# Two layers of cached attention and a token mixer on one core: part of the weights' last query tile as two tiles of 64 rows

## The chip, the cores and the metric

The kernel runs on one core of a Trainium2 chip. The core has a matrix engine (PE, with its weight loads shown as PEld), a vector engine (DVE), an activation engine (ACT), GpSimd (POOL) and a sync engine (SP) that here does nothing but issue DMAs. Sixteen DMA engines bring data from HBM into the on-chip memory (SBUF, 128 partitions). The metric is the device time of one execution in microseconds (us); lower is better.

## The reference

A decode step for a batch of two tokens, in float32, through two identical layers. Each layer is an attention block over a long cache and a small mixer:

```python
def _A_ref(x, k_cache, v_cache, wq, wo):          # x (2, 1, 512)
    # 32 query heads of 128, 8 cached heads, 32768 keys
    q = (lambda x, *d: x.transpose(*d))((x @ wq).reshape(B, Sq, Hq, Dh), 0, 2, 1, 3)
    k = jnp.repeat(k_cache, rep, axis=1)
    v = jnp.repeat(v_cache, rep, axis=1)
    scores = jnp.einsum("bhqd,bhkd->bhqk", q, k) * (Dh ** -0.5)
    p = _softmax(scores, axis=-1)
    o = jnp.einsum("bhqk,bhkd->bhqd", p, v)
    return (lambda x, *d: x.transpose(*d))(o, 0, 2, 1, 3).reshape(B, Sq, Hq * Dh) @ wo
def _B_ref(x, w1, b1, w2, b2):                    # token mixer, 1792 hidden
    h = _layernorm(x, axis=-1)
    u = jnp.einsum("bsd,sf->bdf", h, w1) + b1
    u = _gelu(u)
    y = jnp.einsum("bdf,fs->bds", u, w2) + b2
    return (lambda x, *d: x.transpose(*d))(y, 0, 2, 1)
# both blocks twice, with the same weights and cache
x = x + _A_ref(_layernorm(x, axis=-1), A_k_cache, A_v_cache, A_wq, A_wo)
x = x + _B_ref(_layernorm(x, axis=-1), B_w1, B_b1, B_w2, B_b2)
```

K and V of one batch entry and one cached head are 16 MB each, 512 MB in all, and both layers read the same cache. The weights of one cached head (its four query heads' columns of wq, its rows of wo) are 2 MB.

## The kernel before

**Units.** The work is cut into 32 units (layer, batch entry, cached head). For each unit the kernel makes the query (`make_q`), multiplies it with eight chunks of K (`k_chunk`, L359), finds the maximum, takes exponentials, multiplies with eight chunks of V (`v_chunk`, L492), and adds the result, through wo, to a row sum (`out_1`, `out_2`, L190). A chunk is 2 MB: 128 partitions of 4096 floats. In most of the span K and V come in loads of four chunks, 8 MB; around the two changes of batch entry and layer (some 1000 to 1550 us) the loads are one or two chunks.

**Order.** The function body first writes down, at fixed places in the stream of chunks, which piece of work follows which chunk (`at(time, f, ...)`), and then walks the stream once: load, chunks, pieces that are due. Each engine runs its instructions in that order, so the order of the DMAs in SP's queue is the order in which `load_k` (L344), `load_v` (L446, and L433 for chunks that stay resident) and `load_weights` (L115) are called. Each load is one issue on SP. It waits for what last read or wrote its place in SBUF; whatever stands behind it in SP's queue waits with it.

**Memory.** `mem` holds 13 cells of 4096 floats per partition, and behind them a rest of 5 x 512. Cells 0 to 8 are the ring through which K and V pass: two buffers of four cells for loads of 8 MB. Cells 9 to 12 hold weights. The rest keeps five quads of one V chunk of head 7 between the layers, and at the end one output row.

**Weights.** Heads 5 and 7 are `RESIDENT`: loaded once and kept. The other six, `passing` = 0, 1, 2, 3, 4, 6, are loaded once in each layer. So there are 14 loads: head 0 at the start, the others ten chunks before the first K chunk of the unit that needs them (`at(kbeg[n] - 10, load_weights, ...)`). In the order of SP's queue such a load stands right behind a V load, and the next K load behind it. One load brings 128 rows of 16 KB: four tiles of wq (the 512 inputs as four times 128 partitions, 512 columns each), then four of wo. `wq_at` and `wo_at` give the tiles.

**The query.** `make_q` runs in three steps, two of two matmuls each (L292, the normalized input as the stationary side, one tile of wq as the moving side, 128 rows deep, added up in one PSUM bank) and one that turns the row into columns. The query of a passing head is made for both batch entries at once. The normalized input stands as columns in `xnT`, four for each batch entry, one for each tile of 128 inputs. `first_input` makes them for layer 0 from the loaded input, `to_columns` for layer 1.

Of the kernel before, what the change touches and what calls it, by code (L numbers as in the profile page):

```python
# [10 lines left out]
ALU = mybir.AluOpType  # L11
AX = mybir.AxisListType

P = 128
CK = 4096
# [20 lines left out]
DIRECT = 2  # L36
TAIL_GROUPS = (3, 3, 3, 2, 1)
IDLE = (4, 1, 3, 2)
EPS = 1e-5


@with_exitstack
def gqa_mixer_kernel(ctx: ExitStack, tc: tile.TileContext, x, kt, v, wqo, cols, out):
# [50 lines left out]

# [15 lines left out]
    def wo_at(h):  # L110
        return cells(home[h])[:, W:].rearrange("p (t c) -> p t c", t=R)

    def load_weights(h, cell):
        home[h] = cell
        nc.sync.dma_start(cells(cell), wqo[h])  # L115


    used = [0] * (WCELL0 + WCELLS + 1)
# [63 lines left out]
    def misc():  # L182

        turn[0] += 1
        return small[:, turn[0] % NG * P :][:, :P]
# [13 lines left out]
    def first_input():  # L199

        t = spot()
        cen, sq = (t[:, k * B * DT : (k + 1) * B * DT].rearrange("p (b d) -> p b d", b=B) for k in range(2))
        m, rs = (t[:, (2 * DT + k) * B : (2 * DT + k + 1) * B] for k in range(2))
        p = misc()
        nc.tensor.matmul(p[:, : B * DT], ones, xcols.rearrange("p b d -> p (b d)"), start=True, stop=True)
        nc.vector.tensor_reduce(m, p[:, : B * DT].rearrange("p (b d) -> p b d", b=B), axis=AX.X, op=ALU.add)
# [4 lines left out]
        p = misc()  # L211
        nc.tensor.matmul(p[:, : B * DT], ones, sq.rearrange("p b d -> p (b d)"), start=True, stop=True)
        nc.vector.tensor_reduce(rs, p[:, : B * DT].rearrange("p (b d) -> p b d", b=B), axis=AX.X, op=ALU.add)
        nc.vector.tensor_scalar(rs, rs, 1.0 / D, EPS, op0=ALU.mult, op1=ALU.add)
        nc.gpsimd.tensor_tensor(rs, rs, half_neg.to_broadcast([P, B]), op=ALU.pow)
        for b in range(B):
            xT[b] = xcols[:, b, :]
            nc.vector.tensor_scalar_mul(xnT[:, :, b], cen[:, b, :], rs[:, b : b + 1])  # L218

    *ends, keeper = RESIDENT  # L220
# [30 lines left out]
    def to_columns(key):  # L251

        layer, b = key
        pt = misc()
        for d in range(DT):
            nc.tensor.matmul(  # L256
                pt[:, d : d + 1], ysb[key][:, d * P : (d + 1) * P], ident[:, :1], start=True, stop=True
            )
        nc.vector.tensor_scalar_add(xT[b], pt[:, :DT], b2c)
        mv, rs = stats[key]  # L260
        nc.vector.tensor_scalar(  # L261
            xnT[:, :, b], pt[:, :DT], mv[:, 0:1], rs, op0=ALU.subtract, op1=ALU.mult
        )

    def unit_of(n):

# [10 lines left out]
    def make_q(n, step, place=None):  # L277


        layer, b, h = unit_of(n)  # L280
        both = partner(n)
        m = 1 if both is None else B
        if n in q_kept:
            if step == 2:
                nc.vector.tensor_copy(qpad[n % 2][:, 28 : 28 + R], q_kept.pop(n))
            return
        if step == 0:

            q_ps[n] = pfix.tile([P, 512], F32, name="bcast") if N1 < n <= N3 + 2 else kept[0]
        if step < 2:  # L290
            for d in range(step * DT // 2, (step + 1) * DT // 2):
                nc.tensor.matmul(  # L292
                    q_ps[n][:m, :],
                    xnT[:, d, b : b + m],
                    wq_at(h)[:, d, :],
                    start=(d == 0),
                    stop=(d == DT - 1),
                )
# [234 lines left out]
    def out_2(n):  # L533
        layer, b, h = unit_of(n)
        for r in range(R):
            add_row(r, b, oT[n][:, r, :], wo_at(h)[:, r, :])

    ysb, px = {}, {}
    slope, shift, stats = {}, {}, {}
# [81 lines left out]
    def last_mixer(n):  # L621
# [9 lines left out]
        for k, to in enumerate((kept[1], acc)):  # L631
            for r in range(R):
                nc.tensor.matmul(
                    to[32 * r : 32 * r + 1, :w],
                    oT[n][:, r, 1:],
                    wo_at(h)[:, r, k * w : (k + 1) * w],
                    start=True,
                    stop=True,
                    skip_group_check=True,
                )  # L640
# [81 lines left out]
    def mix_4(key):  # L722

        layer, b = key
        p = px[key]
        nc.tensor.matmul(p, sel[b], ysb[key], start=False, stop=True, skip_group_check=True)
        if layer == LAYERS - 1:
            y = mem[:1, (WCELL0 + WCELLS) * CK :][:, :D]
# [54 lines left out]
    for n in range(NU):  # L783
# [111 lines left out]
def _layout(A_x, A_k_cache, A_v_cache, A_wq, A_wo, B_w1, B_b1, B_w2, B_b2):  # L895

    import numpy as np

    B, HKV, SK, DH = A_k_cache.shape
    D = A_x.shape[-1]  # L900
    n = SK // CK


    keys = np.arange(SK).reshape(n, CK)
    for c0, m in GROUPS:
        keys[c0 : c0 + m] = keys[c0 : c0 + m].reshape(P, m, CK // P).transpose(1, 0, 2).reshape(m, CK)
    k = keys.reshape(n // PACK, PACK // 2, 2, NG, 32, JT // QT, QT // SUB, SUB)
    k = k.transpose(0, 1, 6, 7, 3, 2, 5, 4).reshape(n, CK)
    kt = np.empty((B * HKV, SK * DH), A_k_cache.dtype)
    for u, a in enumerate(A_k_cache.reshape(B * HKV, SK, DH)):  # L910
        for c0, m in GROUPS:
            kt[u, c0 * CK * DH : (c0 + m) * CK * DH] = a[k[c0 : c0 + m].ravel()].T.ravel()
    wq = A_wq.reshape(D // P, P, HKV, -1).transpose(2, 1, 0, 3)
# [4 lines left out]
    return {  # L918
        "x": np.ascontiguousarray(A_x.reshape(B * (D // P), P).T),
        "kt": kt,  # L920
        "v": A_v_cache.reshape(B * HKV, SK * DH),
        "wqo": np.concatenate([wq.reshape(HKV, P, -1), wo.reshape(HKV, DH, -1)], axis=2),
        "cols": np.concatenate(cols, axis=1),
    }

# [24 lines left out]
```

## Time and profile before

| | us |
|---|---|
| three runs: median (lowest to highest) | 2501.64 (2501.58 to 2502.9) |
| the profiled execution: its time | 2501.79 |
| the profiled execution: span from first to last instruction | 2500.0 |
| busy in the span: PE / PEld / DVE / ACT | 1383.1 / 375.5 / 222.4 / 185.4 |
| bytes read from HBM | 1065.91 MB, 426 GB/s over the span |

Lines of the profile name engine, line of the kernel, operation and "out<-in". The letter q behind an engine (SPq) means its sequencer: waits and DMA issues. "PE scores L359 <- DMA mem<-in_kt_dram" is PE at line 359 waiting for a K load; `in_v_dram` is V, `in_wqo_dram` the weights. A wait for several things is put down to the one that came last. "us to landing" is counted from a DMA's issue to its completion.

### The profile page before, as it was taken

Reading aid. Unit: us, or ns where it says so; the run is one execution under the profiler, and the core shown is the slowest. Engines: PE = TensorE matmul, PEld = TensorE weight load, DVE = VectorE, ACT = ScalarE, POOL = GpSimd, SP = SyncE. Lnnn points to the kernel's source line nnn. Section 1 sums busy time; section 2 is a strip of 40 time slices with the busy share of each in tenths; the row PEclk is TensorE's granted clock in tenths of the full one; section 3 lists DMA queues with packets and bytes.
Section 4 is the critical chain, followed back from the end, with each engine's and each line's share of the span. In section 5 each row is a group of like instructions: output and inputs, shape, how many; then the busy total and the mean of one; then the engine's idle time right before and its main releaser. Section 6 shows DMA issues by size and latency. Waiting matters only on the chain.

```text
span 2500.0 us, 20528 instructions
## 1 busy us (share of the span) xinstructions
PE 1383.1 (55%) x9326; PEld 375.5 (15%) x9326; DVE 222.4 (9%) x610; ACT 185.4 (7%) x550; POOL 4.9 (0%) x17
## 2 busy tenths in 40 slices
PE   4545554645445554657667775455546454455546
PEld 1111111111111111111111211111111111111112
DVE  0000000000000000001111110000000000010002
ACT  0000000000000000001012010000000000011002
POOL 0000000000000000000000000000000000000000
PEclk8777777877777777879888977677778777777778
DMA  9999999999999999999999999999999999999996
GB/s 419 436 433 430 433 435 430 436 430 430 433 433 431 434 429 435 425 423 421 426 427 427 423 430 430 432 435 434 432 430 435 435 423 435 433 433 426 432 429 292
DMA packets 31200, 1067.23 MB, mean 427 GB/s; under 512 B 3717, under 2 KB 3721, under 8 KB 4618
## 3 DMA queue, kind: packets, MB, share of 16 engines
q1 hardware_dynamic: 30824, 1065.89, 99.2%
q8 instruction: 73, 1.20, 0.2%
q14 instruction: 13, 0.11, 0.0%
q10 hardware_dynamic: 290, 0.04, 0.0%
HBM read 1065.91 MB, written 0.00 MB: 426 GB/s over the span
## 4 chain that ended last, share of the span: by engine, by line
DMA 74%; PE 24%; issue 0%; DVE 0%; ACT 0%; SPq 0%; POOL 0%; ACTq 0%
DMA mem<-in_v_dram 65%; PE acc L492 19%; DMA mem<-in_kt_dram 9%; PE scores L359 3%; PE bcast L292 1%; PE rows L190 0%; PE small L385 0%; PE small L521 0%; ACT S L714 0%; PE kept L671 0%; PE small L379 0%; PE small L256 0%; ACT mem L681 0%; ACT mem L693 0%; PE bcast L575 0%
## 5 line engine op out<-in xcount | busy, mean ns | idle before, releaser
L359 PE MATMUL scores<-mem,small_sb 128*32 128x512 f32 x4096 | 620.6, 722 | 592.0 <-DMA mem<-in_kt_dram 591.6
L492 PE MATMUL acc<-mem,S 128*16 128x512 f32 x4088 | 614.1, 738 | 468.2 <-DMA mem<-in_v_dram 462.5
L359 PEld LDWEIGHTS scores<-mem,small_sb 128*32 128x32 f32 x4096 | 151.1, 127 | 970.5 <-issue 895.5
L396 ACT ACTIVATE S<-S,small_sb 128x128 f32<-128x128 f32 x240 | 123.5, 519 | 2102.4 <-DVE small_sb L387 1636.6
L492 PEld LDWEIGHTS acc<-mem,S 128*16 128x16 f32 x4088 | 134.8, 110 | 831.7 <-issue 693.2
L369 DVE TENSOR_REDUCE small_sb<-scores 128x1 f32<-128x512 f32 x64 | 44.2, 691 | 874.1 <-PE scores L359 874.1
L391 DVE STREAM_TRANSPOSE S<-scores 128x512 f32<-128x512 f32 x64 | 45.4, 710 | 131.4 <-PE acc L492 131.4
L292 PE MATMUL kept<-mem,small_sb 128*2 128x512 f32 x104 | 50.9, 615 | 1.7 <-DVE small_sb L218 1.7
L190 PE MATMUL rows<-mem,small_sb 128*1 128x512 f32 (+1 forms) x276 | 48.4, 603 | 3.1 <-ACT mem L714 2.4
L396 ACT ACTIVATION_READ_ACCUMULATOR S<-S,small_sb 128x1 f32 x240 | 44.8, 187 | 0.0
L381 DVE TENSOR_REDUCE small_sb<-small 1x4 f32<-1x128 f32 x32 | 8.8, 276 | 280.7 <-PE small L379 280.7
L460 DVE SCALAR_TENSOR_TENSOR S<-acc,small_sb,S 128x128 f32<-128x128 f32 x93 | 32.6, 351 | 3.3
L523 DVE RECIPROCAL small_sb<-small 128x4 f32<-128x4 f32 x32 | 5.9, 185 | 292.1 <-PE small L521 292.1
L531 DVE TENSOR_TENSOR small_sb<-small,small_sb 128x4 f32<-128x4 f32 x31 | 5.1, 164 | 278.2 <-PE small L529 278.2
L714 ACT ACTIVATE S<-bcast,small_sb 128x512 f32<-128x512 f32 x28 | 20.7, 775 | 96.1 <-DVE small_sb L583 82.6
L190 PE MATMUL rows<-S,small_sb 128*1 128x512 f32 (+1 forms) x56 | 21.2, 591 | 8.1 <-ACT S L714 8.1
L304 PE MATMUL small<-small_sb,mem 2*128 2x2 f32 x112 | 15.1, 252 | 17.9 <-DVE mem L301 17.9
L458 DVE TENSOR_SCALAR S<-acc,small_sb 128x128 f32<-128x128 f32 x31 | 10.8, 350 | 128.8 <-PE acc L492 128.8
L292 PE MATMUL bcast<-mem,small_sb 128*1 128x512 f32 (+1 forms) x40 | 19.1, 609 | 1.2 <-DVE small_sb L261 1.2
L529 PEld LDWEIGHTS small<-small_sb,S 128*128 128x128 f32 x62 | 11.6, 234 | 48.8 <-issue 36.0
L304 PEld LDWEIGHTS small<-small_sb,mem 2*128 2x128 f32 x112 | 13.9, 190 | 30.5 <-DVE mem L301 27.3
L529 PE MATMUL small<-small_sb,S 128*128 128x4 f32 x62 | 14.3, 301 | 4.9 <-DVE S L460 4.9
(132 smaller groups left out, 267.7 us busy)
## 6 DMA issues: line engine op xcount, KB each, us to landing
mem<-in_kt_dram SPq DMA_DIRECT2D x44, 2048.0 KB, 12.7
mem<-in_v_dram SPq DMA_DIRECT2D x35, 2048.0 KB, 13.9
mem<-in_v_dram SPq DMA_DIRECT2D x9, 4096.0 KB, 32.7
mem<-in_wqo_dram SPq DMA_DIRECT2D x14, 2048.0 KB, 33.8
mem<-in_kt_dram SPq DMA_DIRECT2D x7, 4096.0 KB, 25.7
mem<-in_v_dram SPq DMA_DIRECT2D x2, 1280.0 KB, 13.6
mem<-in_v_dram SPq DMA_DIRECT2D x2, 768.0 KB, 18.6
mem<-in_v_dram SPq DMA_DIRECT2D x4, 256.0 KB, 28.8
```

The costliest lines, as they stand in the source:

```text
L190: nc.tensor.matmul(rows[32 * g : 32 * g + b + 1, :], weights if b else weights[:, 1:], row, start=False, stop=True, skip_group_check=True,)
L292: nc.tensor.matmul(q_ps[n][:m, :], xnT[:, d, b : b + m], wq_at(h)[:, d, :], start=(d == 0), stop=(d == DT - 1),)
L304: nc.tensor.matmul(pt[:, r * m : (r + 1) * m], q_row[n][:m, r * DH : (r + 1) * DH], ident[:m, :m], start=True, stop=True,)
L359: nc.tensor.matmul(sc_ps[n, half][32 * g : 32 * g + 32, :], q, kc[:, (k * NG + g) * w : (k * NG + g + 1) * w], start=(i == 0 and k == 0), ...
L369: nc.vector.tensor_reduce(mx[n][:, half : half + 1], sc_ps[n, half], axis=AX.X, op=ALU.max)
L391: nc.vector.transpose(S[half], sc_ps[n, half])
L396: nc.scalar.activation(s[:, :, h], s[:, :, h], AF.Exp, bias=neg[n][:, h : h + 1], scale=SCALE, accum_out=lsum[n][:, half, h : h + 1],)
L458: nc.vector.tensor_scalar_mul(t, acc[:, :DH], mask[:, 0:1])
L460: nc.vector.scalar_tensor_tensor(t, acc[:, k * DH : (k + 1) * DH], mask[:, k : k + 1], t, op0=ALU.mult, op1=ALU.add)
L492: nc.tensor.matmul(acc[32 * g : 32 * g + R * QT, :], S[half][:, col : col + R * QT], (own if q < stay else vc)[:, q * w : (q + 1) * w], st ...
L529: nc.tensor.matmul(po[:, :R], asb, selh, start=True, stop=True)
L714: nc.scalar.activation(hid[key, f], px[key], AF.Gelu_apprx_tanh, bias=shift[key][:, f : f + 1], scale=slope[key][:, f : f + 1],)
```

## The change

The last tile of wq (inputs 384 to 511) goes to the end of a head's 16 KB row, so that a row is three tiles of wq, four of wo, one of wq. For the heads in `passing[1:-1]`, 1 to 4, in both layers, the load is split: one load brings the first seven tiles (14 KB of each row) to all 128 partitions; the last tile's rows 0 to 63 and 64 to 127 are loaded as two tiles of 64 rows, both to partitions 0 to 63, the first into the weights' cell, the second into one of the five places of the rest. Each of these is brought by eight loads of 8 rows whose partitions are 4 apart (p, p + 4, ..., p + 28). The other heads' weights are loaded in one piece as before.

The input and the normalized input have a fifth column for each batch entry: inputs 448 to 511 on partitions 0 to 63. The host lays it out for the input, `to_columns` makes it for layer 1 with a further matmul and a further DVE instruction. `make_q` has five matmuls for a split head, the last two 64 rows deep, two in its first step and three in its second.

```diff
+HALF = 64
...
-    widths = dict(x=B * DT, xn=B * DT, q=KEPT_Q * R, cols=4 * FT + 1, ident=P, one=1, half=1, selg=R * QT)
+    widths = dict(x=B * (DT + 1), xn=B * (DT + 1), q=KEPT_Q * R, cols=4 * FT + 1, ident=P, one=1, half=1, selg=R * QT)
...
+    def part(h, k):
+        return cells(home[h])[:, k * D : (k + 1) * D]
+
+    def rest(k):
+        return mem[:, (WCELL0 + WCELLS) * CK :][:, k * D : (k + 1) * D]
+
     def wq_at(h):
-        return cells(home[h])[:, :W].rearrange("p (t c) -> p t c", t=DT)
+        parts = [(P, k, part(h, k)) for k in range(DT - 1)]
+        if not uneven[h]:
+            return parts + [(P, DT - 1, part(h, DT - 1 + R))]
+        return parts + [(HALF, DT - 1, part(h, DT - 1 + R)), (HALF, DT, rest(home[h] - WCELL0))]
...
-    def load_weights(h, cell):
-        home[h] = cell
-        nc.sync.dma_start(cells(cell), wqo[h])
+    def load_weights(h, cell, split=False):
+        home[h], uneven[h] = cell, split
+        n = (DT - 1 + R) * D
+        if not split:
+            nc.sync.dma_start(cells(cell), wqo[h])
+            return
+        nc.sync.dma_start(cells(cell)[:, :n], wqo[h][:, :n])
+        for k, to in enumerate((part(h, DT - 1 + R), rest(cell - WCELL0))):
+            for p in [p + j for p in range(0, HALF, 32) for j in range(4)]:
+                nc.sync.dma_start(to[p : p + 29 : 4], wqo[h][k * HALF + p : k * HALF + p + 29 : 4, n:])
...
+        nc.tensor.matmul(pt[:HALF, DT : DT + 1], ysb[key][:, D - HALF :], ident[:, :1], start=True, stop=True)
         nc.vector.tensor_scalar_add(xT[b], pt[:, :DT], b2c)
         mv, rs = stats[key]
-        nc.vector.tensor_scalar(
-            xnT[:, :, b], pt[:, :DT], mv[:, 0:1], rs, op0=ALU.subtract, op1=ALU.mult
-        )
+        for p, c, n in ((P, 0, DT), (HALF, DT, 1)):
+            nc.vector.tensor_scalar(
+                xnT[:p, c : c + n, b], pt[:p, c : c + n], mv[:p, 0:1], rs[:p], op0=ALU.subtract, op1=ALU.mult
+            )
...
-            for d in range(step * DT // 2, (step + 1) * DT // 2):
+            parts = wq_at(h)
+            for p, d, w in parts[2:] if step else parts[:2]:
                 nc.tensor.matmul(
-                    q_ps[n][:m, :],
-                    xnT[:, d, b : b + m],
-                    wq_at(h)[:, d, :],
-                    start=(d == 0),
-                    stop=(d == DT - 1),
+                    q_ps[n][:m, :], xnT[:p, d, b : b + m], w[:p], start=(d == 0), stop=(d == len(parts) - 1)
                 )
...
-            at(kbeg[n] - 10, load_weights, h, (again if layer else weight_cell)[h])
+            split = h in passing[1:-1]
+            at(kbeg[n] - 10, load_weights, h, (again if layer else weight_cell)[h], split)
...
+    x = np.concatenate([x, np.roll(x[:, :, -1:], HALF, axis=0)], axis=2)
...
-        "wqo": np.concatenate([wq.reshape(HKV, P, -1), wo.reshape(HKV, DH, -1)], axis=2),
+        "wqo": np.concatenate([a.reshape(HKV, P, -1) for a in (wq[:, :, :-1], wo, wq[:, :, -1])], axis=2),
```

`wo_at(h, r)` gives the same four tiles of wo from their new place in the row; its three callers are changed accordingly, and `first_input` reads the first four of the five columns.

More of the change, by code (lines that the diff above doesn't have):

```diff
@@ L105, in cells, with wo_at @@
         return mem[:, k * CK : (k + m) * CK]
+    def part(h, k):
+        return cells(home[h])[:, k * D : (k + 1) * D]
+    def rest(k):
+        return mem[:, (WCELL0 + WCELLS) * CK :][:, k * D : (k + 1) * D]
     def wq_at(h):
-        return cells(home[h])[:, :W].rearrange("p (t c) -> p t c", t=DT)
-    def wo_at(h):
-        return cells(home[h])[:, W:].rearrange("p (t c) -> p t c", t=R)
-    def load_weights(h, cell):
-        home[h] = cell
-        nc.sync.dma_start(cells(cell), wqo[h])
+        parts = [(P, k, part(h, k)) for k in range(DT - 1)]
+        if not uneven[h]:
+            return parts + [(P, DT - 1, part(h, DT - 1 + R))]
+        return parts + [(HALF, DT - 1, part(h, DT - 1 + R)), (HALF, DT, rest(home[h] - WCELL0))]
+    def wo_at(h, r):
+        return part(h, DT - 1 + r)
+    uneven = {}
+    def load_weights(h, cell, split=False):
[8 more added lines that the diff above has]
+                nc.sync.dma_start(to[p : p + 29 : 4], wqo[h][k * HALF + p : k * HALF + p + 29 : 4, n:])
     used = [0] * (WCELL0 + WCELLS + 1)
@@ L201, in first_input, with total @@
         t = spot()
[L202 to L206, printed above, removed]
+        n = B * (DT + 1)
+        cen, sq = (t[:, k * n : (k + 1) * n].rearrange("p (b d) -> p b d", b=B) for k in range(2))
+        m, rs = (t[:, 2 * n + k * B : 2 * n + (k + 1) * B] for k in range(2))
+        def total(dst, src):
+            p = misc()[:, :n]
+            nc.tensor.matmul(p, ones, src.rearrange("p b d -> p (b d)"), start=True, stop=True)
+            by = p.rearrange("p (b d) -> p b d", b=B)[:, :, :DT]
+            nc.vector.tensor_reduce(dst, by, axis=AX.X, op=ALU.add)
+        total(m, xcols)
         nc.vector.tensor_scalar_mul(m, m, 1.0 / D)
@@ L210, in first_input @@
         nc.vector.tensor_mul(sq, cen, cen)
-        p = misc()
-        nc.tensor.matmul(p[:, : B * DT], ones, sq.rearrange("p b d -> p (b d)"), start=True, stop=True)
-        nc.vector.tensor_reduce(rs, p[:, : B * DT].rearrange("p (b d) -> p b d", b=B), axis=AX.X, op=ALU.add)
+        total(rs, sq)
         nc.vector.tensor_scalar(rs, rs, 1.0 / D, EPS, op0=ALU.mult, op1=ALU.add)
@@ L216, in first_input @@
         for b in range(B):
-            xT[b] = xcols[:, b, :]
+            xT[b] = xcols[:, b, :DT]
             nc.vector.tensor_scalar_mul(xnT[:, :, b], cen[:, b, :], rs[:, b : b + 1])
@@ L535, in out_2 @@
         for r in range(R):
-            add_row(r, b, oT[n][:, r, :], wo_at(h)[:, r, :])
+            add_row(r, b, oT[n][:, r, :], wo_at(h, r))
     ysb, px = {}, {}
@@ L635, in last_mixer @@
                     oT[n][:, r, 1:],
-                    wo_at(h)[:, r, k * w : (k + 1) * w],
+                    wo_at(h, r)[:, k * w : (k + 1) * w],
                     start=True,
@@ L727, in mix_4 @@
         if layer == LAYERS - 1:
-            y = mem[:1, (WCELL0 + WCELLS) * CK :][:, :D]
+            y = rest(WCELLS)[:1]
             nc.vector.tensor_scalar_add(y, p[:1, :], b2c[:1, :])
@@ L912, in _layout @@
             kt[u, c0 * CK * DH : (c0 + m) * CK * DH] = a[k[c0 : c0 + m].ravel()].T.ravel()
+    x = A_x.reshape(B, D // P, P).transpose(2, 0, 1)
+    x = np.concatenate([x, np.roll(x[:, :, -1:], HALF, axis=0)], axis=2)
     wq = A_wq.reshape(D // P, P, HKV, -1).transpose(2, 1, 0, 3)
@@ L918, in _layout @@
     return {
-        "x": np.ascontiguousarray(A_x.reshape(B * (D // P), P).T),
+        "x": x.reshape(P, -1),
         "kt": kt,
         "v": A_v_cache.reshape(B * HKV, SK * DH),
-        "wqo": np.concatenate([wq.reshape(HKV, P, -1), wo.reshape(HKV, DH, -1)], axis=2),
+        "wqo": np.concatenate([a.reshape(HKV, P, -1) for a in (wq[:, :, :-1], wo, wq[:, :, -1])], axis=2),
         "cols": np.concatenate(cols, axis=1),
```

## Prediction

> **What bounds the kernel now.** I read the page first: its strip of slices, its DMA queues and its chain.
>
> ```profile
> span 2500.0 us, 20528 instructions
> ...
> DMA  9999999999999999999999999999999999999996
> GB/s 419 436 433 430 433 435 430 436 430 430 433 433 431 434 429 435 425 423 421 426 427 427 423 430 430 432 435 434 432 430 435 435 423 435 433 433 426 432 429 292
> ...
> q1 hardware_dynamic: 30824, 1065.89, 99.2%
> q8 instruction: 73, 1.20, 0.2%
> ...
> DMA 74%; PE 24%; issue 0%; DVE 0%; ACT 0%; SPq 0%; POOL 0%; ACTq 0%
> ```
>
> The DMA engines are busy from the first slice to the last at one rate. Only bytes, or an empty queue, can move the end. The PE parts of the chain are not a second bound; the chain of waits between 200 and 330 us shows what they are:
>
> ```profile
> 217.78 29.28 DMA mem<-in_v_dram
> 247.06 0.14 issue
> 247.20 6.29 PE acc L492 x32
> 253.49 0.32 PE small L521 x2
> 253.81 3.60 PE acc L492 x32
> 257.41 0.02 issue
> 257.43 33.23 DMA mem<-in_v_dram
> 290.66 0.14 issue
> ```
>
> An 8 MB load lands at 247.06, PE reads it until 257.41, and only then SP may issue the load that takes its place. Two such buffers take turns, so at each issue about 10 us of earlier data are still queued. That queue is the cover of everything SP does. How large it is around a weights load is in SP's own timeline, the transfer's row among the DMA issues, and PE's timeline (start, length; idle time before):
>
> ```profile
> 217.78 0.33 SPq L446 DMA_DIRECT2D mem<-in_v_dram  x1
> 218.16 0.43 SPq L115 DMA_DIRECT2D mem<-in_wqo_dram  x1
> 238.29 0.33 SPq L344 DMA_DIRECT2D mem<-in_kt_dram  x1
> ```
> ```profile
> mem<-in_wqo_dram SPq DMA_DIRECT2D x1, 2048.0 KB, 33.8
> ```
> ```profile
> 271.44 4.50 PE L359 MATMUL scores<-mem,small_sb 128*32 128x512 f32 x20 [14.07 <-DMA mem<-in_kt_dram]
> ```
>
> Counting from the landing of the V load (247.06 = 0): the weights land at 218.16 + 33.8 = 251.96, or +4.9; the next K load, issued at -8.8, lands 0.14 us before PE starts on it, at 271.30 or +24.2. So 8 MB take 24.2 - 4.9 = 19.3 us and 2 MB 4.9 us, back to back. SP is idle from 218.6 to 238.3. If the K load's issue came later than the weights' landing, +4.9, the queue would run dry.
>
> **The change part by part.** Eight of the fourteen weights loads are split: heads 1 to 4, in both layers. Each becomes one load of 14 KB a row and sixteen of 8 rows of 2 KB (16 KB each). The bytes stay the same. Seventeen issues stand where one stood, in SP's queue ahead of the K load.
>
> The first cost I look for is a wait. The 214 DMAs share eight completion semaphores, taken in rotation over SP and ACT; the records behind the rows name them. What happens to a ninth issue while the first is in flight is shown once before the change, where short loads crowd (SP's timeline in four windows, then its waits at the ninth and the tenth issue, then the landing of the first and of the second load):
>
> ```profile
> 1097.94 0.33 SPq L446 DMA_DIRECT2D mem<-in_v_dram  x1
> 1098.32 0.42 SPq L433 DMA_DIRECT2D mem<-in_v_dram  x1
> 1100.56 0.33 SPq L446 DMA_DIRECT2D mem<-in_v_dram  x1
> 1100.94 0.91 SPq L433 DMA_DIRECT2D mem<-in_v_dram  x2
> 1102.71 0.33 SPq L446 DMA_DIRECT2D mem<-in_v_dram  x1
> ...
> 1106.03 0.80 SPq L433 DMA_DIRECT2D mem<-in_v_dram  x2
> ...
> 1108.91 0.33 SPq L433 DMA_DIRECT2D mem<-in_v_dram  x1
> ...
> 1113.86 0.33 SPq L344 DMA_DIRECT2D mem<-in_kt_dram  x1
> ```
> ```profile
> SPq L433 <- DMA mem<-in_v_dram: 2.1, 1, 2.1
> ...
> SPq L344 <- DMA mem<-in_v_dram: 4.6, 1, 4.6
> ```
> ```profile
> mem<-in_v_dram SPq DMA_DIRECT2D x1, 2048.0 KB, 11.0
> ...
> mem<-in_v_dram SPq DMA_DIRECT2D x1, 2048.0 KB, 15.5
> ```
>
> The ninth issue (1108.91) goes out as the first load lands (1097.94 + 11.0), the tenth (1113.86) as the second does (1098.32 + 15.5 = 1113.82). It is not a buffer that they wait for: that would end with PE's reading, some 10 us after a landing as above. The record at 1108.91 waits on one semaphore alone, the one that it will itself count up. So an issue waits until the DMA eight issues earlier has landed. With eight loads of 2 MB in flight this costs nothing, for 16 MB are queued. With eight of 16 KB it empties the queue.
>
> Now the steps for one split load, in the same clock. Call the V load before it number 0, the 14 KB load number 1, the small ones 2 to 17, the K load 18.
> - Numbers 1 to 6 go out at once. Number 7 waits for the K load before the V load, one of 8 MB and therefore landed at about -19.3. Number 8 waits for number 0, until 0. Before, SP was free for the K load at -8.8; it is now stuck.
> - Number 9 waits for number 1. That has 14/16 of the bytes: +4.3. This is also when the queue is empty but for a few small rows.
> - Numbers 9 to 17 are nine issues. Spacing of two issues in the rows above: 0.38 (217.78 to 218.16) and 0.91/2 = 0.46. An issue of few rows is shown once, the output at the end (four rows), and the weights' own issue many times:
>
> ```profile
> L702 SPq DMA_DIRECT2D out_dram<-mem x1: 635/635/635, 2497.4 to 2497.4; - x1
> ```
> ```profile
> L115 SPq DMA_DIRECT2D mem<-in_wqo_dram x14: 393/427/438, 0.7 to 1982.8; - x14
> ```
>
>   That gives 0.38 to 0.69 (0.635 and a gap of 0.05) each. I take 0.50, nearer to the loads from SP than to a store of four rows: 4.5 us, so the K load is issued at +8.8. The waits of numbers 10 to 18 for numbers 2 to 10 add nothing if a small load lands within eight issues, 4 us.
> - The K load starts on an empty queue. What that costs is shown at the kernel's start:
>
> ```profile
> 0.74 0.39 SPq L115 DMA_DIRECT2D mem<-in_wqo_dram  x1
> ...
> 28.12 4.47 PE L359 MATMUL scores<-mem,small_sb 128*32 128x512 f32 x25 [7.81 <-DMA mem<-in_kt_dram]
> ```
>
>   The first weights and K load, 10 MB, are issued at 0.74 and have landed at 28.12 - 0.14 = 27.98. Of these 27.2 us 4.9 + 19.3 are bytes; 3.0 are the start and the report of the landing. The other bound is the store of 2 KB at the end, whose landing SP waits for:
>
> ```profile
> SPq L946 <- DMA out_dram<-mem: 0.9, 1, 0.9
> ```
>
>   0.64 + 0.9, about 1.6 us from issue to landing. I take 3.0, since that one is a large load into an empty queue, as here. [...]
>
> So the K load lands at 8.8 + 3.0 + 19.3 = +31.1 where it landed at +24.2: **6.9 us** lost each time, with bounds of 9 x 0.38 + 1.6 - 0.6 = 4.4 and 9 x 0.69 + 3.0 - 0.6 = 8.6 (0.6 is what the shorter first load saves). The next V load is still issued at +10.4 (257.43), when PE frees its buffer, so that it queues behind the K load and nothing is late a second time; but nothing catches up either, as there is no slack in a queue that is always full. The seven other split loads also stand right behind an 8 MB V load. Eight times 6.9 is **55 us**, with bounds of 35 and 69.
>
> The rest is small and covered. Each split head adds one matmul of 64 rows to a query, eight in all, and each of the two layer changes adds a matmul and a subtraction in the column step:
>
> ```profile
> L292 PE MATMUL kept<-mem,small_sb 128*2 128x512 f32 x104 | 50.9, 615 | 1.7 <-DVE small_sb L218 1.7
> ...
> L256 PE MATMUL small<-small_sb,S x16: 250/250/271, 1184.5 to 1379.2; 128*128 128x1 f32 x16
> ...
> L261 DVE TENSOR_SCALAR small_sb<-small,small_sb x2: 272/272/273, 1185.7 to 1379.6; 128x4 f32<-128x4 f32 x2
> ```
>
> 8 x 0.6 = 5 us of PE, which lie in its waits for K loads (14.07 us before the one quoted), and 2 x (0.25 + 0.27) = 1.0 us behind loads already queued; with no cover, 6 us. The queries of the split heads are made two chunks into the K load that follows the weights, 20 us and more after the last small load: no new wait. The wider input has ten columns instead of eight and stands ahead of PE's 7.81 us wait at the start: nothing.
>
> One gain is possible. If a load's rows are dealt to the DMA engines by partition, 64 rows of 2 KB, 128 KB each time, move from one half of the engines to the other: 8 x 16 KB = 128 KB off each of eight engines, and on to each of the other eight. At 4.9 us for 2 MB over sixteen engines (128 KB each) that is 4.9 us of one engine's time. In the sum above I leave it at nothing, since each empty queue lets the faster half wait for the slower anyway. [...]
>
> The profiled execution took 2501.79 us around its span of 2500.0, 0.15 over the median of the runs. 2501.8 + 55 = **2557 us**.
>
> **The rivals.** *It does what it says*: the small loads go out without waiting, sixteen times 0.5 = 8 us in SP's 19.7 us of idle time, and only the shift between engines is left. For it: if one half of the engines is slower, it gets 4.9 us less to do, 2497. Against it: the rows at 1108.91 and 1113.86; and hardly any engine seems to have time to give (a stretch of the span; the last two numbers are the DMA share and GB/s):
>
> ```profile
> 2485.00:2500.00 15.00, 10.49 (x164) 6.41 (x164) 8.60 (x21) 7.57 (x8) 0.54 (x1) 1.00 0.00 1
> ```
>
> After the last load the engines idle for 15 us, which is 0.6% of the span and all that the queues' 99.2% and 0.2% leave free. So a half that finished early would be late elsewhere. If the loads go to the slower half it is 2502 + 4.9 = 2507. Likeliest here: 2500.
>
> *Each small load waits for the one before it*: four neighbouring ones touch interleaved partitions (p, p+4, ... and p+1, p+5, ...); where such ranges are taken as overlapping, three in four of the sixteen issues wait for a landing. Price: twelve round trips of 1.6 to 3.0 us, 19 to 36, and sixteen issues of 0.5, all after +4.3, put the K load's issue at +31 to +48 instead of +8.8; with the 6.9 from above 29 to 46 a load, 8 x 37 = 300, or about 2800. It decides as soon as one small load needs another's landing. For it: strides over partitions stand nowhere in the loads of before, so no row speaks. Against it: buffers that lie side by side in one tile are told apart everywhere in this kernel.
>
> *A cheap stall*: the wait is there, but the issues and the start come at their lower bounds: 2537. This is the low end of my own case.
>
> **How the numbers follow.** The stall by the eight semaphores: 0.83, time 2557, its own range 2537 to 2571 by the bounds, which I widen to 2533 and 2586 for what has no row: a small load that lands later than eight issues (some 1 to 2 us a load), uncovered PE work, the shift of bytes. No wait: 0.10. Waits one by one: 0.07. The two others stay outside the range, 0.17 together. A difference of 0.2% is 5 us, about what a measurement of this kernel tells from no change. The case without a wait falls within it but for its edges: faster 0.02, same 0.07, slower 0.91.
>
> **What would show it.** In the changed kernel SP's waits carry a new row on the line of the small loads, released by the landing of a V load, eight times some 20 us; seventeen issues from SP's first to the K load, the last nine in one run right after the 14 KB load lands; the K load's issue after the V load's landing by about 9 us instead of before it by 9; DMA slices under 9 or rates near 385 GB/s (6.9 of 62.5 us a slice) at eight places; PE's waits for K loads up by about 55 us in all and PE's busy time up by 5. If the K loads behind the split weights are issued before the V load lands, I am wrong in the main point. If they are issued 25 us or more after it, the small loads wait for each other. If the loss is near 35, the empty queue starts faster than at the kernel's beginning.

## The result and the profile after

| | us |
|---|---|
| changed kernel, five runs: median (lowest to highest) | 2572.87 (2572.55 to 2573.4) |
| kernel before, five runs on the same chip | 2501.7 (2501.58 to 2502.9) |
| ratio, 95% interval | 1.0284 (1.0272 to 1.0295) |
| the two profiled executions, after and before | 2573.07 and 2501.79 |

The kernel is slower by 71 us, where the sum of the prediction had 55. The page of the changed kernel: its span, the strip of DMA slices, GB/s, two queues, and the chain that ended last by engine.

```profile
span 2571.3 us, 20747 instructions
...
DMA  9899898998999999999999999899889899999997
GB/s 424 362 437 426 376 438 364 438 435 368 426 437 436 430 433 433 425 427 423 422 426 426 427 430 429 375 431 431 378 361 431 379 429 437 430 435 431 435 429 299
...
q1 hardware_dynamic: 32872, 1065.90, 96.7%
q8 instruction: 73, 1.20, 0.2%
...
DMA 76%; PE 21%; SPq 2%; issue 1%; DVE 0%; ACT 0%
```

The bytes are the same, and so are the rates of most slices. Eight slices are low, one for each split load: four in the first layer, four in the second. The whole loss can be read off them. Their rates add up to 2963 instead of 8 x 432 = 3456 GB/s; a slice is 2571.3/40 = 64.3 us, so the missing bytes are 493/432 x 64.3 = 73 us of a full queue. SPq, which had 0% of the chain before, has 2% of it now.

What happens at one of these places stands in SP's timeline (start, length of the issues with the gaps between them) and in the chain of waits of the changed kernel.

```profile
227.73 0.33 SPq L474 DMA_DIRECT2D mem<-in_v_dram  x1
228.11 0.43 SPq L137 DMA_DIRECT2D mem<-in_wqo_dram  x1
228.59 38.30 SPq L140 DMA_DIRECT2D mem<-in_wqo_dram  x16
266.98 0.38 SPq L372 DMA_DIRECT2D mem<-in_kt_dram  x1
267.46 0.38 SPq L474 DMA_DIRECT2D mem<-in_v_dram  x1
```
```profile
228.11 32.79 DMA mem<-in_wqo_dram
260.90 0.02 issue
260.91 0.62 SPq L140
261.54 0.04 issue
261.58 0.62 SPq L140
...
266.26 0.62 SPq L140
266.88 0.05 issue
...
266.98 0.38 SPq L372
...
267.46 42.10 DMA mem<-in_v_dram
309.56 0.14 issue
```

PE's timeline gives the landings on both sides: PE starts 0.14 us after the data are there.

```profile
256.73 5.05 PE L520 MATMUL acc<-mem,S 128*16 128x512 f32 x32 [8.55 <-DMA mem<-in_v_dram]
...
289.04 5.97 PE L387 MATMUL scores<-mem,small_sb 128*32 128x512 f32 x32 [23.39 <-DMA mem<-in_kt_dram]
```

The V load lands at 256.59, which is again 0. The 14 KB load lands at 260.90, or +4.3. From there on SP issues nine small loads in one run, 0.67 us apart (0.62 and a gap of 0.04), and the K load goes out at 266.98, +10.4, on an empty queue. It lands at 288.90, +32.3, where it landed at +24.2 before: **8.1 us lost**. The next V load is issued right behind it and lands at 309.56, 20.66 us after it. Before, the V load in this place came 290.66 - 271.30 = 19.36 us after its K load: another 1.3 us.

SP's and PE's waits of the changed kernel (total, times, longest), PE's wait of the kernel before, and the 62.5 us around this place (the last two numbers are the DMA share and GB/s) say the same in sums.

```profile
SPq L140 <- DMA mem<-in_v_dram: 150.2, 8, 19.0
...
SPq L140 <- DMA mem<-in_kt_dram: 48.3, 8, 9.5
...
SPq L140 <- DMA mem<-in_wqo_dram: 29.3, 8, 3.8
```
```profile
PE scores L387 <- DMA mem<-in_kt_dram: 659.9, 85, 23.4
```
```profile
PE scores L359 <- DMA mem<-in_kt_dram: 591.6, 79, 15.1
```
```profile
249.90:312.40 62.50, 26.57 (x164) 7.09 (x165) 2.64 (x8) 1.89 (x8) 0.00 (x0) 0.71 0.88 373
```

Three waits of SP stand on the line of the small loads, eight times each: for the K load before the V load, for the V load, for the 14 KB load. PE waits 659.9 us for K loads where it waited 591.6, 68 us more. Its waits for V loads fell by 9 us (from 462.5 to 453.3) and its busy time rose by 11, so that the three together give 70 of the 71 us.

### The profile page after: what moved, and what is told of

It is laid out like the page before. It is cut to its first block, busy times and chain, and to the rows that moved or that the text cites. A ratio compares the mean times of both kernels' runs of the same rounds, so it can differ in the third digit from the quotient of the medians.

```text
span 2571.3 us, 20747 instructions
## 1 busy us (share of the span) xinstructions
PE 1394.0 (54%) x9346; PEld 374.9 (15%) x9346; DVE 223.0 (9%) x612; ACT 185.4 (7%) x550; POOL 4.9 (0%) x17
## 4 chain that ended last, share of the span: by engine, by line
DMA 76%; PE 21%; SPq 2%; issue 1%; DVE 0%; ACT 0%
DMA mem<-in_v_dram 44%; DMA mem<-in_kt_dram 22%; PE acc L520 13%; DMA mem<-in_wqo_dram 9%; PE scores L387 6%; SPq L140 2%; PE bcast L324 1%; PE kept L324 0%; PE rows L215 0%; PE small L413 0%; PE small L549 0%; PE kept L699 0%; SPq L372 0%; PE small L332 0%; PE small L407 0%
## 5 line engine op out<-in xcount | busy, mean ns | idle before, releaser
L387 PE MATMUL scores<-mem,small_sb 128*32 128x512 f32 x4096 | 612.9, 723 | 660.3 <-DMA mem<-in_kt_dram 659.9
L520 PE MATMUL acc<-mem,S 128*16 128x512 f32 x4088 | 609.0, 733 | 461.4 <-DMA mem<-in_v_dram 453.3
L324 PE MATMUL kept<-mem,small_sb 128*2 128x512 f32 (+1 forms) x120 | 58.6, 612 | 1.7 <-DVE small_sb L247 1.7
L742 ACT ACTIVATE S<-bcast,small_sb 128x512 f32<-128x512 f32 x28 | 20.7, 774 | 99.1 <-DVE small_sb L611 81.3
L215 PE MATMUL rows<-S,small_sb 128*1 128x512 f32 (+1 forms) x56 | 20.9, 592 | 7.1 <-ACT S L742 7.1
L486 DVE TENSOR_SCALAR S<-acc,small_sb 128x128 f32<-128x128 f32 x31 | 10.9, 350 | 128.3 <-PE acc L520 128.3
```

The costliest lines, as they stand in the source:

```text
L215: nc.tensor.matmul(rows[32 * g : 32 * g + b + 1, :], weights if b else weights[:, 1:], row, start=False, stop=True, skip_group_check=True,)
L324: nc.tensor.matmul(q_ps[n][:m, :], xnT[:p, d, b : b + m], w[:p], start=(d == 0), stop=(d == len(parts) - 1))
L387: nc.tensor.matmul(sc_ps[n, half][32 * g : 32 * g + 32, :], q, kc[:, (k * NG + g) * w : (k * NG + g + 1) * w], start=(i == 0 and k == 0), ...
L520: nc.tensor.matmul(acc[32 * g : 32 * g + R * QT, :], S[half][:, col : col + R * QT], (own if q < stay else vc)[:, q * w : (q + 1) * w], st ...
L742: nc.scalar.activation(hid[key, f], px[key], AF.Gelu_apprx_tanh, bias=shift[key][:, f : f + 1], scale=slope[key][:, f : f + 1],)
```

## The experiments

Eleven kernels, each timed beside the kernel before (its medians lay between 2501.7 and 2501.97). All are the changed kernel with another way of loading the last tile of wq of a split head. "K issue" is when the next K load goes out, counted from the landing of the V load, and "V after K" how long after that K load the next V load lands, both at the second split load of the profile, the place shown above.

| kernel | loads per split head, of them behind the V load | K issue | V after K | median us | ratio (95%) |
|---|---|---|---|---|---|
| before | 1, 1 | -8.8 | 19.4 | 2501.7 | 1 |
| changed | 17, 17 | +10.4 | 20.7 | 2572.9 | 1.0284 (1.0272 to 1.0295) |
| three | 3, 3 | -8.9 | 19.4 | 2521.3 | 1.0080 (1.0067 to 1.0094) |
| seven | 7, 7 | +0.1 | 19.4 | 2520.1 | 1.0071 (1.0058 to 1.0083) |
| eight | 8, 8 | +5.3 | 20.5 | 2529.1 | 1.0108 (1.0094 to 1.0122) |
| spread4 | 17, 5 | -9.8 | 19.4 | 2514.0 | 1.0046 (1.0033 to 1.0060) |
| whole2 | 2, 2 | -8.2 | 19.4 | 2504.0 | 1.0009 (1.0000 to 1.0018) |
| spread4c | 17, 5 | -8.5 | 19.4 | 2525.9 | 1.0097 (1.0083 to 1.0110) |
| pool16 | 17, 1 on SP | -9.5 | 19.4 | 2510.9 | 1.0039 (1.0026 to 1.0051) |
| wide17 | 17, 17 | +10.5 | 20.9 | 2575.6 | 1.0296 (1.0282 to 1.0310) |
| cols7 | 7, 7 | +0.1 | 19.4 | 2507.5 | 1.0022 (1.0013 to 1.0031) |
| cols8 | 8, 8 | +4.5 | 20.4 | 2525.9 | 1.0096 (1.0082 to 1.0110) |
| near17 | 17, 17 | +7.5 | 20.4 | 2550.3 | 1.0191 (1.0174 to 1.0208) |

The theory was that an issue waits for the landing of the DMA eight issues earlier, and that this empties the queue. The first rival was that the small loads wait for each other, the second that many small loads, or this shape of them, cost something by themselves.

**Few loads, and the step from seven to eight.** In `three` each tile of 64 rows comes in one load:

```diff
-            for p in [p + j for p in range(0, HALF, 32) for j in range(4)]:
-                nc.sync.dma_start(to[p : p + 29 : 4], wqo[h][k * HALF + p : k * HALF + p + 29 : 4, n:])
+            nc.sync.dma_start(to[:HALF], wqo[h][k * HALF : (k + 1) * HALF, n:])
```

> The same two tiles of 64 rows, but each brought by one load of 64 rows: three loads for a head's weights instead of seventeen. Semaphore theory (an issue waits until the DMA eight issues earlier has landed): the K load waits for a load that landed long before, the queue never empties, 2502 us (2498 to 2507). Rival, the half-partition destination or the extra matmuls cost the time: it stays near 2573. Rival, SP's issue time alone: also about 2502, as only two issues are added.

In `seven` and `eight` four strided loads stay, and the rest is brought in two or three loads; in `seven` the K load is the eighth DMA after the V load, in `eight` the ninth:

```diff
-        for k, to in enumerate((part(h, DT - 1 + R), rest(cell - WCELL0))):
...
+        to = part(h, DT - 1 + R)
+        for j in range(4):
+            nc.sync.dma_start(to[j : j + 29 : 4], wqo[h][j : j + 29 : 4, n:])
+        for a, b in ((32, 64),):
+            nc.sync.dma_start(to[a:b], wqo[h][a:b, n:])
+        nc.sync.dma_start(rest(cell - WCELL0)[:HALF], wqo[h][HALF:, n:])
```

> Seven loads for a head's weights: the 14 KB load, four of 8 rows 4 partitions apart, one of 32 rows, one of 64 rows. Semaphore theory: the K load is the eighth issue after the V load and waits for the V load's landing; 4.9 us of weights are then still queued, more than the start of a load takes (2.6 us), so nothing is lost: 2502 us (2499 to 2507). Rival, the shape of the 8-row loads costs: sixteen of them cost 71 us, so the four here cost about 18, 2519. Rival, issue time on SP that holds the K load: 7 issues of at most 0.67 us fit in SP's idle 19.7 us, 2502.

(`eight` has `((32, 48), (48, 64))` in that loop.)

> As with seven loads, but the load of 32 rows is cut into two of 16 rows: eight loads, the same bytes in the same places. Semaphore theory: the K load is now the ninth issue after the V load and waits for the 14 KB load's landing at +4.3 us; it lands at 4.35 + 21.95 = 26.3 instead of 24.2 us, 2.1 us lost each time, 17 us in all, and up to 7 more from realigned DMA engines: 2519 to 2526. Both rivals, shape and issue time: the same as seven loads within 5 us (8 x 0.67).

Measured: 2521.3, 2520.1 and 2529.1. The times of `three` and `seven` missed by 18 to 19 us, though their K issues came as the theory says: in `three` before the V load's landing, in `seven` 0.06 us after it. In `eight` the K issue moved to the landing of the 14 KB load, but the step from `seven` cost 9.0 us where 17 to 24 were expected. The traces show why: in `seven` the K load already lands 25.6 to 26.8 us after the V load instead of 24.2, as it does in `three` without any late issue, and the wait of `eight` moves it only to 26.7 to 27.6. So this pair does not give the price of the wait. SP's timeline of `eight`:

```profile
222.91 0.43 SPq L137 DMA_DIRECT2D mem<-in_wqo_dram  x1
223.38 2.67 SPq L140 DMA_DIRECT2D mem<-in_wqo_dram  x4
226.10 5.95 SPq L142 DMA_DIRECT2D mem<-in_wqo_dram  x2
251.09 0.53 SPq L143 DMA_DIRECT2D mem<-in_wqo_dram  x1
256.32 0.35 SPq L374 DMA_DIRECT2D mem<-in_kt_dram  x1
```

The four strided loads of neighbouring, interleaved partitions go out in one run of 2.67 us, and so do nine of them in the changed kernel: no small load waits for another's landing, so the first rival falls. `seven` came out at its rival's price for the 8-row shape, 2519, but `three` has no load of that shape and costs as much. With no late issue at all and three loads, `three` is 19 us slower than the kernel before: something other than waits costs time.

**The same small loads without the wait.** `spread4` issues the sixteen loads of the change in four groups of four, each behind another 8 MB load; `pool16` issues them from GpSimd:

```diff
+            if split:
+                for i, k in enumerate((22, 18, 14, 10)):
+                    at(kbeg[n] - k, load_few, h, (again if layer else weight_cell)[h], i)
```

> All sixteen 8-row loads of each split head are kept, but issued four at a time behind four successive K and V loads, the last four right after the 14 KB load. Semaphore theory: the waits for the DMA eight issues earlier end before the next buffer is free, the queue never empties; what is left is 128 KB more on each of eight DMA engines and 128 KB less on the other eight, -4.9 to +4.9 us: 2497 to 2507. Rivals, the loads' shape or their issue time: about 2573 as in the changed kernel.

```diff
-                nc.sync.dma_start(to[p : p + 29 : 4], wqo[h][k * HALF + p : k * HALF + p + 29 : 4, n:])
+                nc.gpsimd.dma_start(to[p : p + 29 : 4], wqo[h][k * HALF + p : k * HALF + p + 29 : 4, n:])
```

> The changed kernel with the sixteen small loads issued from GpSimd; SP keeps the 14 KB load and the K load. If the loss is SP standing still for semaphores that the small loads took: the K load is issued before the V load lands and the time falls to about 2514, the level of the spread loads. Rival, a burst of sixteen small loads costs the DMA engines the time itself: near 2573. If GpSimd's loads share the eight semaphores, the K load waits as before: near 2573 too, and SP's waits show it.

Measured: 2514.0 and 2510.9. SP's timeline of `spread4`, then of `pool16`, then the strip of `spread4`'s page:

```profile
220.93 0.33 SPq L477 DMA_DIRECT2D mem<-in_v_dram  x1
221.30 0.43 SPq L137 DMA_DIRECT2D mem<-in_wqo_dram  x1
221.78 10.27 SPq L144 DMA_DIRECT2D mem<-in_wqo_dram  x4
240.02 0.33 SPq L375 DMA_DIRECT2D mem<-in_kt_dram  x1
```
```profile
221.11 0.33 SPq L474 DMA_DIRECT2D mem<-in_v_dram  x1
221.49 0.43 SPq L137 DMA_DIRECT2D mem<-in_wqo_dram  x1
242.02 0.33 SPq L372 DMA_DIRECT2D mem<-in_kt_dram  x1
```
```profile
DMA  9999999999999999999999999999999999999996
```

The K load goes out about 20 us after the V load, as before the change, and the slices are full again. With the same bytes in the same sixteen pieces the stall is gone, and with it 59 (`spread4`) to 62 us (`pool16`) of the 71. The 9 to 12 us that remain over the kernel before are put down to the loads themselves; they are more than the 2497 to 2507 that `spread4` was given. In neither kernel is there a burst any more: in `pool16` no wait of SP is released by a small load, and half of GpSimd's issues stand some 4 us or more apart. So these two do not tell the wait from a burst's own cost; `cols8` below, without a burst of sixteen, does.

**What costs time in the loads.** `whole2` brings the last tile in one load of 128 rows, to all partitions; `spread4c` is `spread4` with eight neighbouring partitions a load; `wide17` cuts each tile of 64 rows in eight pieces of 64 columns, so that each load spans 64 partitions:

```diff
+        uneven[h] = False
+        nc.sync.dma_start(part(h, DT - 1 + R), wqo[h][:, n:])
```

> The last tile is loaded by itself, but in one load of 128 rows of 2 KB to all 128 partitions; the query uses it as before the change. Two loads for a head's weights. If the 19 us of the three-load version come from writing 256 KB to half of the partitions: 2502 us (2499 to 2506). Rival, rows of 14 KB and 2 KB cost more than rows of 16 KB: about 2521.

```diff
-            nc.sync.dma_start(to[p : p + 29 : 4], wqo[h][k * HALF + p : k * HALF + p + 29 : 4, n:])
+            nc.sync.dma_start(to[p : p + 8], wqo[h][k * HALF + p : k * HALF + p + 8, n:])
```

> The sixteen loads spread over four places as in the run before, but each brings 8 rows to 8 neighbouring partitions instead of partitions 4 apart. If it matters which partitions are written at one time, as the 19 us of the three-load version suggest: more than the 2514 of the spread loads, up to 2521. Rival, each small load costs eight DMA engines a fixed 0.21 us whatever its partitions: 2514 (2511 to 2517).

```diff
+            for c in range(0, D, HALF):
+                nc.sync.dma_start(to[:HALF, c : c + HALF], wqo[h][k * HALF : (k + 1) * HALF, n + c : n + c + HALF])
```

> The changed kernel with each tile of 64 rows cut by columns: eight loads of 64 rows of 256 bytes instead of eight of 8 rows of 2 KB, still seventeen loads. Semaphore theory: the K load still waits for nine issues after the 14 KB load has landed, each about 0.47 us (as other loads of 64 and more rows) instead of 0.67, so it goes out at +8.5 instead of +10.4 us: 8 x 1.8 = 14 us less than the changed kernel, 2556 to 2562. Rival, the 8-row shape on eight engines is what costs: 2521, as with three loads.

Measured: 2504.0, 2525.9 and 2575.6. Cutting the row costs 2.3 us (`whole2`), so `three` owes its other 17 us to bringing both halves of the tile to partitions 0 to 63: 17.4/8 = 2.2 us more for each 256 KB, whose bytes alone take 0.6 at 19.36 us for 8 MB. The traces agree: the K load behind lands 25.6 to 27.2 us after the V load in `three` and 24.3 to 24.4 in `whole2`, 15.7 us over the eight places. The third load by itself is not the reason, as five further loads cost 3.5 us together in `cols7` below. Loads to eight neighbouring partitions (`spread4c`) cost twice what loads 4 apart cost (24 us against 12), and more than the 2521 that was expected at most. So which partitions a load writes counts in both pairs of runs, and what makes it count no run here shows.

`wide17` missed by 14 us and more: its issues took 0.60 us (the row below) where 0.47 with the gap was expected, its 14 KB load landed at +4.8 instead of +4.3, and so its K load went out as late as that of the changed kernel.

**The step from seven to eight, without the half.** `cols7` and `cols8` cut the tile of `whole2` by columns, into six and seven loads to all 128 partitions:

```diff
+        uneven[h] = False
+        cuts = (0, 64, 128, 192, 256, 384, 512)
+        for a, b in zip(cuts, cuts[1:]):
+            nc.sync.dma_start(part(h, DT - 1 + R)[:, a:b], wqo[h][:, n + a : n + b])
```

> The last tile goes to all 128 partitions (as in the two-load version, 2504 us), but in six pieces by columns: seven loads for a head's weights. Semaphore theory: the K load is the eighth issue after the V load and goes out when the V load lands, with 4.9 us of weights still queued: 2504 us (2501 to 2509). Rival, every further load costs the queue a fixed time: 5 loads x 8 x 0.2 us = 8 us, 2512.

> As with seven loads to all 128 partitions, the last tile in seven pieces by columns: eight loads. Semaphore theory: the K load waits for the 14 KB load's landing at +4.3 us and lands at 4.35 + 21.95 = 26.3 instead of 24.2 us, 2.1 us lost each time, 17 in all, and up to 7 more for the V load behind it after an emptied queue: 17 to 24 us above the seven-load version, 2521 to 2528. Rival, no part is played by the eighth load: within 2 us of the seven-load version.

Measured: 2507.5 and 2525.9. SP's timelines of `cols7` and of `cols8`:

```profile
219.90 0.33 SPq L474 DMA_DIRECT2D mem<-in_v_dram  x1
220.28 0.42 SPq L137 DMA_DIRECT2D mem<-in_wqo_dram  x1
220.75 8.04 SPq L141 DMA_DIRECT2D mem<-in_wqo_dram  x6
247.87 0.33 SPq L372 DMA_DIRECT2D mem<-in_kt_dram  x1
```
```profile
221.87 0.33 SPq L474 DMA_DIRECT2D mem<-in_v_dram  x1
222.25 0.43 SPq L137 DMA_DIRECT2D mem<-in_wqo_dram  x1
222.72 28.25 SPq L141 DMA_DIRECT2D mem<-in_wqo_dram  x7
255.12 0.33 SPq L372 DMA_DIRECT2D mem<-in_kt_dram  x1
```

In `cols7` the V load lands at 219.90 + 27.91 = 247.81 and the K load, eight issues behind it, goes out at 247.87; the 14 KB load is still in the queue, and the late issue costs next to nothing. In `cols8`, with the same bytes and one load more, the V load lands at 250.63, the K load waits for the 14 KB load until 255.12, and the queue is empty. One load more is worth 18.4 us. This is the wait alone, with no strides, no half of the partitions and few issues.

**The time of an issue.** `near17` is the changed kernel, its burst of sixteen loads kept, with eight neighbouring partitions a load instead of eight that are 4 apart:

```diff
-            for p in [p + j for p in range(0, HALF, 32) for j in range(4)]:
-                nc.sync.dma_start(to[p : p + 29 : 4], wqo[h][k * HALF + p : k * HALF + p + 29 : 4, n:])
+            for p in range(0, HALF, 8):
+                nc.sync.dma_start(to[p : p + 8], wqo[h][k * HALF + p : k * HALF + p + 8, n:])
```

> The changed kernel with the sixteen small loads bringing 8 rows each to 8 neighbouring partitions; such issues took 0.29 us in the spread version, against 0.62 us for 8 partitions 4 apart. Semaphore theory with the issue as its second term: nine issues of 0.34 us, gap included, put the K load's issue at 4.3 + 3.1 = +7.4 instead of +10.4 us after the V load's landing, and its landing at 7.4 + 21.95 = +29.3 instead of +32.3: 8 x 3.0 = 24 us less than the changed kernel, 2549 us (2545 to 2555). Rival, the issues do not set the end of the stall: 2573, or more, since neighbouring partitions cost the DMA engines more (2526 against 2514 when spread).

Measured: 2550.3, 22.6 us faster than the changed kernel. The rows of the small loads' line (lowest, median, highest length of an issue in ns) in the changed kernel, in `near17` and in `wide17`:

```profile
L140 SPq DMA_DIRECT2D mem<-in_wqo_dram x128: 623/624/779, 57.4 to 2001.2; - x128
```
```profile
L140 SPq DMA_DIRECT2D mem<-in_wqo_dram x128: 272/293/410, 57.9 to 1978.8; - x128
```
```profile
L140 SPq DMA_DIRECT2D mem<-in_wqo_dram x128: 465/595/652, 58.1 to 2002.5; - x128
```

Shorter issues bring the K issue from +10.4 to +7.5 and its landing from +32.3 to +29.4: 2.9 us a load, 23 us in all. These are the loads that were the dearer ones in `spread4c`. In the burst that does not show: from K issue to landing both kernels take 21.9 us.

No version beats the kernel before. `whole2`, the cheapest, stands 0.1% above it; the difference is small, but its eleven runs (2503.49 to 2505.4) all lie above the fifteen of the kernel before (2501.27 to 2503.22).

## Why the prediction was right in kind and 16 us short

- **The wait.** As predicted in every step: the three releasers, the landing of the 14 KB load at +4.3, nine issues in one run behind it, no wait of one small load for another, eight places. `cols7` against `cols8`, and `pool16` and `spread4` against the changed kernel, show that the wait belongs to the DMA eight issues earlier and that the empty queue is its price. In the records of the changed kernel the small loads issued at 256.61, at 260.91 and after it each wait on one semaphore alone, the one that they then count up themselves. (The 214 DMAs of the prediction are SP's loads; with the store and ACT's three there are 218.)
- **The issues: the term that was mis-sized.** The prediction took 0.50 us each out of bounds of 0.38 and 0.69, "nearer to the loads from SP than to a store of four rows". They take 0.67. The shape of the transfer decided: with another shape of the same sixteen loads the issue took 0.29 us (`near17`). The row of 635 ns for the store of a few rows was the nearer one. Nine issues are 6.1 us instead of 4.5: 1.6 us a load, 13 us in all. `near17` shows this term by itself.
- **The start on an empty queue.** Taken as 3.0 us; measured 288.90 - 266.98 - 19.36 = 2.6, which takes 3 us off the sum. This lies between the prediction's two bounds, the 3.0 of the kernel's start and the 1.6 of the store of 2 KB.
- **The K load.** With both terms it is late by 8.1 us instead of 6.9 (inside the bounds of 4.4 and 8.6), and 8 x 8.1 = 65.
- **"Nothing is late a second time".** This was wrong: the V load behind the late K load takes 20.7 instead of 19.4 us. In the records of the landings it takes 20.4 to 20.8 us at seven of the eight places and 19.4 at one; before, one of these eight took 20.6 us, one 19.6 and the others 19.4. The difference is 7 us in all. By the same records the K loads land 8.0 to 8.3 us later, 64.5 in all. So 55 + 13 - 3 + 7 = 72, where the two spans differ by 71.3.
- **PE.** Busy time rose by 10.9 us instead of 5: a float32 matmul stands as two instructions in the trace, and so there are sixteen more of 0.59 us in the queries (120 where 104 stood) and not eight. It lay under waits for K loads, as predicted, and cost nothing.
- **The shift between the engines, put at nothing.** The sum above closes without it. In the records each small load's semaphore is counted up once, 1.04 to 1.17 us after the issue begins, and eight times more when the data have come, where that of a load of 128 rows is counted up sixteen times. Which DMA engines bring the eight rows, and whether they are eight, no run shows: the 4.9 us that the prediction and `spread4` let the shift gain or lose rest on the author's assumption that rows go to the engines by partition. `spread4` took 2514.0, above the whole range of 2497 to 2507.
- **The rivals.** Without the wait (`spread4`, `pool16`) the change costs 9 to 12 us, not the -2 that "does what it says" was given: that case had a shift of bytes between the engines, but not that loads to half of the partitions cost more than their bytes. "Each waits for the one before it" is out by the runs of issues 0.67 us apart. The cheap stall fails at its lowest issue time.

**The second lateness and what stays open.** A load of 128 rows lands when the last of sixteen counts on its semaphore has come: at the place above the last count of the K load stands at 288.90, and PE starts 0.14 us after it. Before the change the sixteen counts of a K load behind a split head's place lie 1.9 to 3.9 us apart; in the changed kernel, where this load starts on an empty queue, they come within 0.7 us. Of the V load behind it fifteen counts come within 0.7 us too, and where it is late, one alone comes 1.1 to 1.4 us after them.

The queue q8 carries instructions, 73 packets in the span at 0.2% x 16 x 2571.3/73 = 1.1 us each. Five kernels (changed, `eight`, `wide17`, `cols8`, `near17`) let a K load start on an empty queue, at 40 places. At 33 of them a q8 packet starts between the landing of the K load and that of the V load, and the V load takes 20.2 to 20.9 us (in the changed kernel at seven of its eight places, 20.4 to 20.8). At the other seven there is none, and it takes 19.3 to 19.4 (in the changed kernel at one, 19.36). The DMA queues in two such stretches of the changed kernel, 1932.07 to 1952.65 (20.58 us) and 1840.37 to 1859.73 (19.36 us):

```profile
q1 hardware_dynamic: 144, 8.39, 94.2%
q8 instruction: 1, 0.02, 0.3%
```
```profile
q1 hardware_dynamic: 144, 8.39, 100.0%
```

So the reading, with each of the sixteen counts taken as one DMA engine's, is that the packet holds up one of them, which shows only when all sixteen have just started level: before the change a packet falls into six of the eight stretches, and four of these V loads still take 19.4 us. It fits at all 40 places, but no run took the packets away: the cause is not shown by an experiment.

## What to carry to other kernels

Where a queue is kept full by a few large loads, count the DMAs and not only the bytes: in this kernel each DMA waits for the landing of the one eight issues earlier, so that seven loads between two large ones cost 6 us in all and an eighth 18 more. If small pieces are needed, spread them over several large loads (2514.0 us here against 2572.9) or give them to an engine whose queue holds nothing urgent (2510.9), and let each span all 128 partitions (2504.0 in `whole2` against 2521.3 in `three`). When a burst does empty the queue, the time of one issue becomes a price (0.29 us an issue instead of 0.62 saved 22.6 us), and it has to be read from an issue of the same shape.

## What the runs showed of the hardware

- **An issue's length on SP depends on its shape**: 0.29 us for 8 neighbouring rows of 2 KB (`near17`, `spread4c`), 0.43 for 128 rows of 14 KB, 0.60 for 64 rows of 256 B in `wide17`, 0.62 for 8 rows that are 4 partitions apart.
- **What is short to issue can be slow to carry out.** On a full queue the 8 neighbouring rows cost 24 us in all, the 8 rows 4 apart 12; in the burst the order is turned round, 2550 against 2573.
- **The loads of both halves to partitions 0 to 63 cost more than their bytes**: in `three` 2.2 us for each 256 KB beyond the 0.6 that they take at the rate of the large loads.
- **After an empty queue the load behind the next one is slower by 0.8 to 1.5 us when an instruction packet falls into it**: at 33 of 40 places, against 19.3 to 19.4 us at the seven without a packet. In the table all five kernels whose K load was issued after the 14 KB load's landing have 20.4 to 20.9 in the column "V after K", the others 19.4.
